# Last value rows over ACT in one transfer, the first value unit whole before the transposes, tiles copied by two engines

## The chip, the cores and the metric

One core of one Trainium2 chip. The metric is the device time of one execution in microseconds (us), as the median of several executions. The profile's own span is some 1.7 us shorter than that time (147.1 against 148.78 us for the profiled execution of the kernel before). I compare spans with spans and times with times.

Engines: PE is TensorE (PEld its weight loads), DVE is VectorE, ACT is ScalarE, POOL is GpSimd, SP is the engine that issues most transfers. PSUM is the memory that PE's results stand in until DVE or ACT copies them out.

## The reference

A token-wise gate mixes a linear attention branch and a feed-forward branch over 2048 tokens of width 448:

```python
g = sigmoid((x * gate_w).sum(-1, keepdims=True))
q, k, v = split_heads(x @ wqkv)                      # 16 heads of 28
phi_q = concat(softmax(q @ w_phi), softmax(-(q @ w_phi)))   # per head; phi_k from k in the same way
o = (phi_q @ (phi_k.T @ v)) / (phi_q @ phi_k.sum(tokens) + 1e-6)
a = o @ wo
b = gelu(x @ w1 + b1) @ w2 + b2
out = g * a + (1 - g) * b
# ... all inputs bfloat16; shapes: wqkv 448x1344, w_phi 16x28x28, w1 448x1792, w2 1792x448
```

## The kernel before

Only the first 14 us matter here. The value weights `WvG` (448 rows) are held as four chunks of 128 partitions; the last 64 rows are loaded twice, once into each half of chunk 3, because each half of the partitions serves one of two matmuls that run beside each other. The first 512 tokens of x are loaded as they are, in two blocks, and turned on PE (`turn`); everything else is turned by transposing transfers from SP. The key weights arrive transposed (`WkT`), are multiplied with a block matrix `bd` made of `w_phi` (`key_chunk`), and the result is the weight of the key units.

```python
nc.sync.dma_start(x0[:, 0:2, :], two[0])                       # first x block
nc.scalar.dma_start(WvG[:, 0:3, 0:D], ...)                     # value weights, 336 KB
nc.sync.dma_start(wphi[:, 0:3, :], ...)
nc.scalar.dma_start(wphi[0:HP, 3, :], wflat[384:448, :])       # HP = 64
nc.sync.dma_start(x0[:, 2:4, :], two[1])                       # second x block
# ...
for i in range(2):                                             # last value rows, into both halves
    nc.gpsimd.dma_start(WvG[i * HP:(i + 1) * HP, 3, 0:D], A_wqkv[384:448, 2 * D:3 * D])
# ...
load_wT(WkT, D, 0, 256)                                        # transposing transfers from SP
load_wT(WkT, D, 256, D)
load_x(512, 512)
load_wT(WqT, 0)
load_x(1024, 512)
# ...
turn(0, 1, nc.vector.tensor_copy, 0, 2)      # 4 PE transposes into PSUM, then one copy to xT
turn(0, 2, nc.scalar.copy, 2, 4)
turn(2, 0, nc.vector.tensor_copy)
idle(2, P)
v0a, v0b = V(0, 3), V(1, 0)                  # the first two value units: 6 full matmuls each
v0a.un.full(0, True, False)                  # 3 matmuls
v0a.un.full(1, True, False, cs=(0,))         # 1 matmul
turn(1, 1, nc.vector.tensor_copy)            # these two need the second x block
turn(3, 2, nc.scalar.copy)
for m in range(4):
    heads_map(m)                             # bd, on DVE
v0a.un.full(1, True, False, cs=(1, 2))       # the 2 matmuls left over
v0b.un.fulls(True, False)                    # needs tile 1, then tile 3
# ...
key_chunk(0, 1, nc.scalar.copy)              # needs WkT's first part and bd
key_chunk(1, 2, nc.scalar.copy)
v0a.un.rest(False, True)                     # needs the last value rows
v0b.un.rest(False, True)
key_chunk(2, 1, nc.vector.tensor_copy)       # needs WkT's second part
# ... the rest of the kernel
```

The softmax here doesn't subtract the row's maximum and nothing guards it: scores larger than these inputs give would overflow.

## Time and profile before

| | kernel before |
|---|---|
| time, median of 4 runs | 148.59 us (148.47 to 148.67) |
| span of the profiled execution | 147.1 us |
| PE busy | 97% |
| second x block: data moved / landed | 5.42 / 6.22 us |
| key weights' first / second part landed | 7.12 / 8.44 us |
| key weights' product starts on PE | 8.33 us |

"Landed" is the moment at which the last of the sixteen increments of a transfer's semaphore is recorded, one increment from each of the 16 DMA engines; that is what a waiting engine sees. The prediction shows the lines on which the argument rests. One view is added here: the busy times in stretches of 1 us. Its columns are the stretch, its length, the busy time of each engine, the granted clock, the mean busy share of the 16 DMA engines (packets that overlap are counted more than once, so it can exceed 1), and GB/s.

```profile
5.00:6.00 1.00, 0.82 (x4) 0.20 (x2) 0.09 (x1) 0.00 (x0) 1.00 (x1) 1.00 1.17 193
6.00:7.00 1.00, 0.73 (x10) 0.56 (x10) 0.30 (x1) 0.08 (x1) 1.00 (x3) 1.00 1.28 279
7.00:8.00 1.00, 1.00 (x7) 0.46 (x6) 0.95 (x5) 0.51 (x1) 1.00 (x2) 1.00 1.18 173
```

The DMA engines are busy all through these 3 us and move 173 to 279 GB/s.

### The profile page before, as it was taken

Reading aid. Unit: us, or ns where it says so; the run is one execution under the profiler, and the core shown is the slowest. Engines: PE = TensorE matmul, PEld = TensorE weight load, DVE = VectorE, ACT = ScalarE, POOL = GpSimd, SP = SyncE. Lnnn points to the kernel's source line nnn. Section 1 sums busy time; section 2 is a strip of 40 time slices with the busy share of each in tenths; the row PEclk is TensorE's granted clock in tenths of the full one; section 3 lists DMA queues with packets and bytes.
Section 4 is the critical chain, followed back from the end, with each engine's and each line's share of the span. In section 5 each row is a group of like instructions: output and inputs, shape, how many; then the busy total and the mean of one; then the engine's idle time right before and its main releaser. Section 6 shows DMA issues by size and latency. Waiting matters only on the chain.

```text
span 147.1 us, 3117 instructions
## 1 busy us (share of the span) xinstructions
PE 142.9 (97%) x1293; PEld 78.5 (53%) x1293; DVE 82.5 (56%) x140; ACT 64.8 (44%) x73; POOL 72.0 (49%) x59
## 2 busy tenths in 40 slices
PE   7899999999999999999999999999999999999992
PEld 4554645554566666964444445554555555545561
DVE  0342999997999992179993002721637747044112
ACT  4266987889999877326777762000000000000000
POOL 7932499898889999200699940000621110024000
PEclk9999999999999999999999999999999999999999
DMA  4999857449999999997159990340313623303111
GB/s 129 266 184 224 199 123 150 108 85 241 224 221 223 366 246 145 181 153 139 38 98 171 100 206 0 71 76 2 125 31 85 87 69 71 71 4 125 60 34 31
DMA packets 46190, 18.98 MB, mean 129 GB/s; under 512 B 36800, under 2 KB 46016, under 8 KB 46176
## 3 DMA queue, kind: packets, MB, share of 16 engines
q1 hardware_dynamic: 45392, 18.23, 61.8%
q10 hardware_dynamic: 624, 0.43, 0.9%
q8 instruction: 10, 0.16, 0.5%
q0 software_dynamic: 160, 0.12, 0.3%
q14 instruction: 4, 0.03, 0.1%
HBM read 6.34 MB, written 1.84 MB: 56 GB/s over the span
## 4 chain that ended last, share of the span: by engine, by line
PE 94%; DMA 3%; SPq 1%; DVE 0%; issue 0%
PE hp L478 29%; PE y L577 28%; PE q_ps L231 6%; PE y L194 6%; PE k_ps L231 4%; PE v_ps L194 3%; DMA gel<-in_A_x_dram 3%; PE v_ps L231 3%; PE kv L490 3%; PE nm L502 2%; PE k_ps L205 2%; PE k_ps L194 2%; PE w_ps L316 1%; PE y L211 1%; PE q_ps L194 1%; PE v_ps L211 1%
## 5 line engine op out<-in xcount | busy, mean ns | idle before, releaser
L577 PE MATMUL y<-w_sb,gel 128*128 128x448 bf16 (+1 forms) x224 | 43.8, 349 | 0.0
L478 PE MATMUL hp<-xT,w_sb 64*128 64x512 bf16 x224 | 42.7, 376 | 0.0
L478 PE MATMUL hp<-xS,w_sb 64*128 64x512 bf16 x168 | 40.1, 376 | 0.0
L482 ACT ACTIVATE gel<-hp,b1T 128x1024 bf16<-128x1024 f32 x28 | 30.8, 1115 | 13.6 <-PE hp L478 13.0
L478 PEld LDWEIGHTS <-w_sb 64*128 64x128 bf16 x392 | 22.9, 94 | 19.1
L577 PEld LDWEIGHTS <-gel 128*128 128x128 bf16 x238 | 22.3, 98 | 19.3 <-issue 0.4
L538 POOL TENSOR_SCALAR b2u<-b2b,ungate 128x448 f32<-128x448 bf16 x16 | 10.0, 642 | 40.2 <-DVE res L589 40.2
L259 POOL TENSOR_TENSOR gel<-gel,rec 128x1792 bf16<-128x1792 bf16 x8 | 25.6, 3214 | 2.2 <-DVE rec L258 2.2
L589 DVE SCALAR_TENSOR_TENSOR res<-y,ungate,b2u 128x448 bf16<-128x448 f32 (+1 forms) x16 | 10.3, 673 | 25.0 <-PE y L577 13.2
L259 POOL TENSOR_TENSOR phiq<-phiq,rec 128x1792 bf16<-128x1792 bf16 x4 | 12.7, 3211 | 11.0 <-DVE rec L258 11.0
L256 DVE TENSOR_REDUCE sums<-gel 128x64 f32<-128x1792 bf16 x8 | 16.0, 2002 | 0.0
L250 ACT ACTIVATE gel<-k_ps 128x896 bf16<-128x896 f32 x16 | 13.7, 922 | 3.5 <-PE k_ps L231 2.1
L509 DVE TENSOR_SCALAR den<-nm,enL 128x16 f32<-128x16 f32 x16 | 3.6, 228 | 17.0 <-PE nm L502 17.0
L231 PEld LDWEIGHTS <-xT 64*128 64x128 bf16 x112 | 9.2, 94 | 5.6 <-issue 0.4
L259 POOL TENSOR_TENSOR phqT<-phqT,rec 128x1792 bf16<-128x1792 bf16 x3 | 11.3, 3808 | 0.0
L515 DVE TENSOR_TENSOR o_all<-nm,den 128x448 bf16<-128x448 f32 (+2 forms) x24 | 11.0, 485 | 0.6
L231 PE MATMUL q_ps<-gel,xT 64*128 64x448 bf16 (+1 forms) x56 | 10.1, 349 | 0.0
L231 PEld LDWEIGHTS <-xS 64*128 64x128 bf16 x84 | 7.8, 94 | 3.8
L258 DVE RECIPROCAL rec<-sums 128x64 f32<-128x64 f32 x16 | 8.9, 553 | 1.1
L231 PE MATMUL q_ps<-phqT,xS 64*128 64x448 bf16 (+1 forms) x42 | 9.1, 349 | 0.0
L278 DVE CAST vaug<-v_ps 128x896 bf16<-128x896 f32 x7 | 7.5, 1070 | 2.7 <-PE v_ps L194 2.4
L194 PE MATMUL y<-wo_sb,phiq 128*128 128x448 bf16 (+1 forms) x36 | 8.2, 349 | 0.0
(96 smaller groups left out, 146.4 us busy)
## 6 DMA issues: line engine op xcount, KB each, us to landing
w_sb<-in_B_w_dram SPq DMA_DIRECT2D x4, 784.0 KB, 10.8
out_dram<-res SPq DMA_DIRECT2D x15, 112.0 KB, 1.7
w_sb<-in_B_w_dram SPq DMA_DIRECT2D x2, 560.0 KB, 13.6
xS<-xT SPq DMA_DIRECT2D x8, 96.0 KB, 2.3
phqT<-gel SPq DMA_DIRECT2D x4, 168.4 KB, 3.4
gel<-in_A_x_dram SPq DMA_DIRECT2D x2, 224.0 KB, 3.6
w_sb<-in_B_w_dram SPq DMA_DIRECT2D x1, 448.0 KB, 10.2
gel<-in_A_wqkv_dram ACTq DMA_DIRECT2D x1, 336.0 KB, 3.7
```

The lines of the kernel that those rows point to most:

```text
L194: nc.tensor.matmul(o, lhsT=self.L(i, slice(0, P), c), rhs=self.R(slice(0, P), c)[:, n0:n1], start=(first and c == 0), stop=(last and c == 2))
L231: nc.tensor.matmul(o, lhsT=tok, rhs=(W if direct else SWAPPED[name])[rows, c, 0:n], start=(k == 0), stop=own)
L250: nc.scalar.activation(out=o, in_=src, func=ACT.Exp, scale=(1.0, -1.0)[s])
L256: nc.vector.reduce_sum(out=sums[:], in_=ph, axis=AX.X)
L258: nc.vector.reciprocal(out=rec[:], in_=sums[:])
L259: eng.tensor_tensor(out=ph, in0=ph, in1=rec[:, :, :, None].to_broadcast([P, 32, 2, DH]), op=ALU.mult)
L478: nc.tensor.matmul(hp[:, i, :].rearrange("p (b t) -> p b t", b=2), lhsT=w1_sb[i * HP:(i + 1) * HP, k, j * P:(j + 1) * P], rhs=x_half(i, k, ...
L482: nc.scalar.activation(out=dst, in_=hp[:].rearrange("p i (b t) -> p i b t", b=2), func=ACT.Gelu_apprx_tanh, bias=b1T[:, j:j + 1])
L515: nc.vector.tensor_tensor(out=o_tok[:, col:col + (b - a) * DH].rearrange("p (q j d) -> p q j d", j=2, d=DH), in0=nm[:, a // 2:b // 2, 0:56 ...
L538: nc.gpsimd.tensor_scalar(out=b2u[t][:], in0=b2b[:], scalar1=ungate[:, place(t):place(t) + 1], scalar2=0.0, op0=ALU.mult, op1=ALU.add)
L577: nc.tensor.matmul(o, lhsT=gel[:, j, tok], rhs=w2_sb[:, j, n0:n1], start=(first and j == 0), stop=(last and j == NJ - 1))
L589: nc.vector.scalar_tensor_tensor(out=res[t][:, n0:n1], in0=o, scalar=ungate[:, e:e + 1], in1=b2u[t][:, n0:n1], op0=ALU.mult, op1=ALU.add)
```

## The change

The intent: take two transfers (1.3 us of issuing) off POOL by loading the last value rows twice in one transfer from ACT; fill the wait for the second x block with the two value matmuls that stood behind it; and have each of the two tiles that come with that block copied out of PSUM by DVE and ACT together, so that the second value unit can start sooner. Moved along with it: b1's small load and one SP issue less for `wo`.

```diff
@@ -119,6 +119,9 @@
     wflat = A_w_phi.rearrange("h a b -> (h a) b")
     nc.sync.dma_start(wphi[:, 0:3, :], wflat[0:384, :].rearrange("(c p) b -> p c b", p=P))
     nc.scalar.dma_start(wphi[0:HP, 3, :], wflat[384:448, :])
+    nc.scalar.dma_start(WvG[:, 3, 0:D],
+                        bass.AP(tensor=A_wqkv.tensor, offset=A_wqkv.offset + 384 * 3 * D + 2 * D,
+                                ap=[[0, 2], [3 * D, HP], [1, D]]))
     nc.sync.dma_start(x0[:, 2:4, :], two[1])
 
     def load_wT(W, base, r0=0, r1=D):
@@ -144,8 +147,6 @@
     nc.gpsimd.memset(ones[:], 1.0)
     nc.gpsimd.affine_select(out=ident[:], in_=ones[:], pattern=[[-1, P]],
                             compare_op=ALU.is_equal, fill=0.0, base=0, channel_multiplier=1)
-    for i in range(2):
-        nc.gpsimd.dma_start(WvG[i * HP:(i + 1) * HP, 3, 0:D], A_wqkv[384:448, 2 * D:3 * D])
     on4 = ones[:, 0:64].rearrange("p (c h) -> p c h", c=4)
     nc.gpsimd.affine_select(out=hm[:], in_=on4, pattern=[[P, 4], [-DH, 16]],
                             compare_op=ALU.is_ge, fill=0.0, base=0, channel_multiplier=1)
@@ -154,6 +155,7 @@
     nc.gpsimd.dma_start(gb[0:3, :], gate_w[0:384].rearrange("(c p) -> c p", p=P))
     nc.gpsimd.dma_start(gb[3:4, :].rearrange("o (i p) -> o i p", i=2),
                         gate_w[None, None, 384:448].to_broadcast([1, 2, HP]))
+    nc.gpsimd.dma_start(bb[0:NJ, :], B_b1.rearrange("(j p) -> j p", p=P))
     pk4 = phik.rearrange("p t (q m) -> p (t q) m", m=HP)
     nc.gpsimd.memset(pk4[:, :, 56:64], 0.0)
     nc.gpsimd.memset(vaug[:, :, :, 56:58], 1.0)
@@ -161,7 +163,6 @@
     nc.gpsimd.memset(pq4[:, :, 56:64], 0.0)
     pq4 = phiq[:].rearrange("p t (q m) -> p (t q) m", m=HP)
     nc.gpsimd.memset(pq4[:, :, 56:64], 0.0)
-    nc.gpsimd.dma_start(bb[0:NJ, :], B_b1.rearrange("(j p) -> j p", p=P))
 
     load_wT(WkT, D, 0, 256)
     load_wT(WkT, D, 256, D)
@@ -334,27 +335,28 @@
         for c in range(c0, c1):
             dlo = (0, 2, 1, 3)[j] * D + (c * P if c < 3 else (384 if j < 2 else 320))
             nc.tensor.transpose(tp[:, 0, c * P:(c + 1) * P], x0f[:, dlo:dlo + P], ident[:])
-        copy(out=xT[:, c0:c1, j * P:(j + 1) * P],
-             in_=tp[:, 0, c0 * P:c1 * P].rearrange("p (c t) -> p c t", t=P))
-
-    turn(0, 1, nc.vector.tensor_copy, 0, 2)
-    turn(0, 2, nc.scalar.copy, 2, 4)
-    turn(2, 0, nc.vector.tensor_copy)
+        for i, eng in enumerate(copy):
+            a, b = c0 + i * (c1 - c0) // len(copy), c0 + (i + 1) * (c1 - c0) // len(copy)
+            eng(out=xT[:, a:b, j * P:(j + 1) * P], in_=tp[:, 0, a * P:b * P].rearrange("p (c t) -> p c t", t=P))
+
+    both = (nc.vector.tensor_copy, nc.scalar.copy)
+    turn(0, 1, both[:1], 0, 2)
+    turn(0, 2, both[1:], 2, 4)
+    turn(2, 0, both[:1])
     idle(2, P)
     v0a, v0b = V(0, 3), V(1, 0)
-    v0a.un.full(0, True, False)
-    v0a.un.full(1, True, False, cs=(0,))
+    v0a.un.fulls(True, False)
+
     def heads_map(m):
         h0, h1 = HEADS[m]
         nc.vector.tensor_tensor(out=bd[:, m, 0:(h1 - h0) * DH].rearrange("p (h d) -> p h d", d=DH),
                                 in0=wphi[:, m, None, :].to_broadcast([P, h1 - h0, DH]),
                                 in1=hm[:, m, h0:h1, None].to_broadcast([P, h1 - h0, DH]), op=ALU.mult)
 
-    turn(1, 1, nc.vector.tensor_copy)
-    turn(3, 2, nc.scalar.copy)
+    turn(1, 1, both)
+    turn(3, 2, both)
     for m in range(4):
         heads_map(m)
-    v0a.un.full(1, True, False, cs=(1, 2))
     v0b.un.fulls(True, False)
     low_half(512, nc.gpsimd)
     twin(WqT, nc.gpsimd.tensor_copy)
@@ -422,8 +424,7 @@
         for i in range(2):
             f = slice(h * F // 2, (h + 1) * F // 2)
             nc.sync.dma_start(w1_sb[i * HP:(i + 1) * HP, :, f], B_w1[:, f].rearrange("(k p) f -> p k f", p=HP))
-    for c0, c1 in ((0, 1), (1, 3)):
-        nc.sync.dma_start(wo_sb[:, c0:c1, :], A_wo[c0 * P:c1 * P, :].rearrange("(c p) n -> p c n", p=P))
+    nc.sync.dma_start(wo_sb[:, 0:3, :], A_wo[0:384, :].rearrange("(c p) n -> p c n", p=P))
     for i in range(2):
         nc.sync.dma_start(wo_sb[i * HP:(i + 1) * HP, 3, :], A_wo[384:448, :])
     for j0, j1 in ((0, 5), (5, 10), (10, NJ)):
```

## The prediction

> **What bounds the kernel now.** I read the busy table first, then TensorE's (PE's) list of waits, then the chain that ended last, and only then the first 14 us of the timeline.
>
> ```profile
> PE 142.9 (97%) x1293; PEld 78.5 (53%) x1293; DVE 82.5 (56%) x140; ACT 64.8 (44%) x73; POOL 72.0 (49%) x59
> ...
> PE w_warm L322 <- PEq L640: 0.8, 1, 0.8
> PE tp L336 <- DMA gel<-in_A_x_dram: 0.4, 1, 0.4
> ```
>
> The first line is the busy table: PE is busy 97% of the span. The other two are all of PE's waits: the start, and 0.4 us for the second block of x before its transposes. Afterwards PE never waits for long enough to be listed, so a microsecond won or lost before about 14 us should reach the end of the kernel whole, unless a transfer further on takes it back. The chain says where such a microsecond can come from:
>
> ```profile
> 1.73 4.49 DMA gel<-in_A_x_dram
> 6.22 0.05 issue
> 6.27 0.62 PE tp L336 x8
> 6.88 1.61 PE v_ps L194 x8
> 8.49 0.46 PE w_ps L316 x8
> 8.95 0.48 PE v_ps L211 x4
> 9.44 0.34 PE w_ps L316 x4
> ```
>
> Columns are start, length, what. Until 6.22 us the chain is the second x transfer; from 6.27 it is PE alone: 8 transposes, 8 value matmuls (2 left of the first value unit, 6 of the second), the key weights' product for chunks 0 and 1 (w_ps), the last value rows (L211), then chunk 2. Details from the timeline:
>
> ```profile
> 4.89 0.93 PE L194 MATMUL v_ps<-gel,xT 128*128 128x448 bf16 x4
> 6.70 0.42 DVE L337 COPY xT<-tp 128x512 bf16<-128x512 bf16 x1 [1.61 <-PE tp L336]
> 6.92 0.59 ACT L337 COPY xT<-tp 128x512 bf16<-128x512 bf16 x1 [2.32 <-PE tp L336]
> 7.18 0.87 PEld L194 LDWEIGHTS <-xT 128*128 128x128 bf16 x6 [0.36 <-DVE xT L337]
> ```
>
> and from the list of transfers (size of one, us from issue to landing):
>
> ```profile
> gel<-in_A_wqkv_dram ACTq DMA_DIRECT2D x1, 336.0 KB, 3.7
> gel<-in_A_wqkv_dram POOLq DMA_DIRECT2D x2, 56.0 KB, 4.6
> gel<-in_A_wqkv_dram SPq DMA_TRANSPOSE x3, 4.9
> ```
>
> Value matmuls start about every 0.19 us (1.15 us for 6). Those of the first unit that stand before the transposes start at 4.89, 5.09, 5.28 and 5.47; a fifth could start at 5.66, but the transposes wait until 6.27. So the hole is 0.6 us of issue time, though the list shows 0.4, as it counts from the modelled end. The second unit starts at 7.18, when VectorE's (DVE's) whole-tile copy is done; the two left-over matmuls fill most of that wait. The last three lines are the bulk of the value weights over ACT, their last rows in two transfers over GpSimd (POOL), the transposed loads over SP. Of the latter the first two bring the key weights: issued at 2.25 and 3.7 they land at 7.1 and 8.4 (the landing events of the trace), for uses at 8.33 (chunk 0) and 9.37 (chunk 2). They have only 1.2 and 0.9 us to spare.
>
> **What the Trainium skill says.** (1) "DMA: Bandwidth & Descriptors", section "Issuing engines are not separate DMA queues": transfers from any issuer run on the same 16 DMA engines, so another issuer saves only the issuer's time. The trace agrees in that the 2 POOL transfers (1.34 us of POOL to issue) move their data in the midst of the second x block. (2) The same page, "Why a DMA increments its semaphore by 16 and not by 1": a transfer is spread over the largest k up to 16 that divides the slowest dimension (not of size 1) of both its access patterns, and one issued from SP or ACT takes the lowest-numbered k engines; "Rules for kernel authors" warns that a leading zero-stride broadcast of c copies confines a transfer to at most c engines. The new transfer is just that: its source as built is 2 copies (stride 0) of 64 rows, so k would be 2. No transfer from SP or ACT before has such a pattern, so this trace neither supports nor contradicts it. (3) "Queues, rings and completion order" there: an engine takes turns between the queues packet by packet. The trace records each 896-byte row as one packet (41 ns) and each transposed piece as a 256-byte packet (18 ns). (4) "TensorE: Matmul & The Clock Gate", Part 1: the clock drops only after an idle window of about 3.4 us. The granted clock is full here throughout, and the waits I expect are 1 us or less, so I count no clock loss.
>
> **The change part by part.**
> - *First value unit whole before the transposes.* Two matmuls (2 x 0.19 = 0.38 us) move into the 0.6 us hole. They issue until 6.04, so if x still lands at 6.22 the transposes still start at 6.27.
> - *Two engines per tile.* DVE's half tile is 256 columns: 0.29 us, as its copy of that size at 4.02 took, in place of 0.42. The copy of tile 1 starts 0.43 after the transposes' start T (6.27 to 6.70), so the second unit can start at T+0.43+0.29+about 0.07, i.e. T+0.79, against T+0.91. But the built program makes ACT's half wait for DVE's half of the same tile, not for PE. So the halves run one after the other: ACT's half (0.37 us, as at 4.23) ends at T+0.43+0.29+0.06+0.37, or T+1.15. The third matmul, which needs it, wants to go at T+0.79+0.38 = T+1.17: about 0.05 us late. Six matmuls end at about T+1.99; with T = 6.27 the key product could start at 8.26 in place of 8.33: **gain 0.07 us**. The head maps on DVE (0.91 us for 4) start at T+1.0, and the last one they delay is just in time.
> - *Last value rows from POOL to ACT.* This takes 112 KB out of the middle of the second x block. 112 KB at the 200 to 340 GB/s that the stretches from 3 to 6 us moved is 0.3 to 0.5 us, so x could land by 5.9 and T become 6.04: **another 0.23 us at most**. Together 0.1 to 0.3 us, if nothing else came of it.
> - *The other side of the same transfer.* With k = 2, two engines carry 64 rows each: 64 x 41 ns = 2.6 us, against 0.3 us (two POOL packets of 0.16) before. The SP transposes need all 16 engines, and the engines are nearly full from 5 us on. The first key transpose has 64 packets per engine; taking turns one for one with 64 rows costs it up to 2.6 us on these two engines, less the 0.3 saved and about 0.2 of idle time. It would land at about 7.1+2.1 = 9.2, the second at 8.4+2.1 = 10.5. The key product then starts at about 9.25, not 8.33: **+0.9 us**. Chunks 0 and 1 and the last rows take 1.04 us, so chunk 2 wants to start at 10.3 and waits to about 10.55: **+0.25 more**. Net of all, PE is 1.15 us later than before. Later transfers come about 2 us later on those engines too, but had more room: x's next block is first used at 13.0 after landing at 11.0, the query weights 2.3 us after 13.28, and both uses move by 1.15 as well.
> - *gate and b1 first, wo in one transfer.* POOL's head masks and small loads come 1.3 us sooner; gate's first use on PE is at 11.1, b1's at 17.7. wo is not used on PE before 99 us. One SP issue less of about 0.6 us. All hidden: 0.
>
> **The rivals.**
> - *A: the two-engine spread hits the key weights*, as summed: 148.55+1.15 = 149.7, say 149.3 to 150.2. For it: the pattern as built, the 0.9 and 1.2 us of spare time, the full engines. Against: nothing in this trace shows a spread of 2.
> - *B: the transfer is spread over 16 after all* (the pattern being turned round somewhere, or the destination's 128 rows deciding). Then only the gains remain: 148.55-0.07 to -0.3, i.e. 148.2 to 148.5. For it: the destination alone would give 16.
> - *C: spread over 2 but hidden*, the transposes going first and the rows creeping behind. Then the last value rows land late; they are wanted at 8.9, ahead of chunk 2, and would come at 8 to 10: 148.4 to 149.5. The PE wait then sits at L211's rows and not at w_ps.
> - *D: backlog*: the two loaded engines hold back later blocks (x at 13, the query weights at 15.5) more than the PE delay covers: 150.2 to 151.5.
>
> **How the range follows.** A 0.5, B 0.3, C 0.12, D 0.08. The middle of that mixture is about 149.5; from B's good half to A's bad end gives 148.2 to 150.3. None of these gets to 2% (below 145.6 or above 151.5), except a bad D. So within 2% has 0.95; faster 0.01, slower 0.04.
>
> **What the profile of the changed kernel would show.** A: PE's waits gain a wait of 0.7 to 1.2 us at w_ps for a DMA from wqkv, the key transposes' time to landing grows from 4.9 to about 7, and the new ACT transfer takes 6 us or more to land. B: that transfer lands within 5 us and the only PE wait left is 0.2 us or less at the transposes or the second value unit. In both: six value matmuls before the transposes, the transposes at 6.0 to 6.3, DVE's half copies at 0.29 us, and ACT's halves starting only after DVE's. From 23 us on every stretch should be as long as before, merely shifted; a difference there would make the working wrong even if the total were right. A landing of x much later than 6.3 would mean that the rows collide with x rather than with the transposes.

## The result, and the profile after

The changed kernel takes **150.43 us** (median of 4 runs, 150.12 to 150.80) against 148.59 us before: it is slower by 1.25% (ratio 1.0125, 95% interval 1.0101 to 1.0150). The prediction said 149.5 with a range up to 150.3, so the time fell just outside. "Within 2%" held.

The busy table of the kernel after, and then PE's waits (who waited for what: us in total, times, longest):

```profile
PE 143.6 (97%) x1293; PEld 74.6 (50%) x1293; DVE 85.3 (57%) x141; ACT 64.8 (44%) x74; POOL 70.5 (47%) x57
```

```profile
PE tp L337 <- DMA gel<-in_A_x_dram: 1.2, 1, 1.2
PE w_warm L323 <- PEq L641: 0.8, 1, 0.8
PE v_ps L195 <- DVE xT L340: 0.2, 1, 0.2
```

The busy table alone says nothing: PE is at 97% as before. The list of waits tells where to look: the wait for the second x block grew from 0.4 to 1.2 us, and a small wait for DVE's copy appeared. There is no wait for the key weights, which the prediction had named as the place: they landed at 9.51 us, 0.4 us before PE came to them (9.90). The chain that ended last, after:

```profile
1.73 6.17 DMA gel<-in_A_x_dram
7.91 0.05 issue
7.95 0.41 PE tp L337 x4
8.36 0.02 issue
8.39 0.30 DVE xT L340
8.69 0.05 issue
8.73 1.33 PE v_ps L195 x6
10.07 0.46 PE w_ps L317 x8
```

The x transfer, issued at the same 1.73, lands at 7.91 instead of 6.22. From there to the key product (10.07 against 8.49 in the chain's reckoning) the chain is 0.1 us shorter than before. The product is 1.58 us late, and the span 1.5 us longer (148.6 against 147.1). Later stages add nothing: from the first hidden-layer matmul to PE's last it is 103.4 us before (40.91 to 144.29) and 103.3 us after (42.49 to 145.82).

The stretches that answer to those of before:

```profile
5.00:6.00 1.00, 1.00 (x4) 0.33 (x4) 0.09 (x1) 0.00 (x0) 1.00 (x3) 1.00 3.34 83
6.00:7.00 1.00, 0.78 (x4) 0.21 (x2) 0.00 (x0) 0.00 (x0) 1.00 (x2) 1.00 0.14 47
7.00:8.00 1.00, 0.05 (x1) 0.05 (x2) 0.00 (x0) 0.00 (x0) 0.56 (x1) 1.00 1.13 98
```

Here is the loss. Between 6 and 7 us the DMA engines are busy to 0.14 of 16, which is about 2 engines, and move 47 GB/s where they moved 279 before. The 3.34 in the stretch before is no high load: it counts packets in full where they start, and 24 packets of the key weights' transposed load, which start between 5.06 and 5.61 us, take 1.6 to 2.2 us each (the trace's packet records; they end between 7.17 and 7.31, and 18 ns is usual). The packet records do not name the engine, but 0.14 of 16 engines and the late increments below fit one reading: fourteen engines stand still with a transposed packet in hand, and two work.

The list of transfers, after (size, us to landing):

```profile
gel<-in_A_wqkv_dram ACTq DMA_DIRECT2D x1, 336.0 KB, 3.7
gel<-in_A_wqkv_dram ACTq DMA_DIRECT2D x1, 112.0 KB
gel<-in_A_wqkv_dram SPq DMA_TRANSPOSE x3, 6.2
```

The new 112 KB transfer has no time to landing, because its semaphore does not count in sixteen single steps. The trace has three updates for it: one at 3.28 us, before any of its rows had moved, and one each at 8.39 and 8.70. Two engines did the work, as the prediction had expected from the pattern. Its 128 rows, one packet each, moved between 4.71 and 8.05 us.

And the x block: its last data packet ended at 5.14 us, even sooner than before (5.42). Its sixteen increments came at 5.15 and 5.25 us from two engines, and between 7.60 and 7.91 from the other fourteen. **The bytes had been there for 2.8 us before PE was told so.** The trace also has sixteen packets of 4 bytes on SP's queue between 4.57 and 5.14 us, as many as there are increments. If these are the writes of the increments, as their number and place suggest, even they had been started by then.

From the timeline, after, the parts that went as planned (start, length, engine, line, operation; in brackets the idle time before and what ended it):

```profile
4.89 1.88 PE L195 MATMUL v_ps<-gel,xT 128*128 128x448 bf16 x6
8.39 0.51 DVE L340 COPY xT<-tp 128x256 bf16<-128x256 bf16 x2 [3.30 <-PE tp L337]
8.71 0.65 ACT L340 COPY xT<-tp 128x256 bf16<-128x256 bf16 x2 [4.10 <-DVE xT L340]
```

Six value matmuls stand before the transposes. The copies are halves, and ACT's start only when DVE's first half is done. (That six matmuls took 1.88 us and not 1.3 is told in the next section but one.)

### The profile page after: what moved, and what is told of

It is laid out like the page before. It is cut to its first block, busy times and chain, and to the rows that moved or that the text cites. A ratio compares the mean times of both kernels' runs of the same rounds, so it can differ in the third digit from the quotient of the medians.

```text
span 148.6 us, 3116 instructions
## 1 busy us (share of the span) xinstructions
PE 143.6 (97%) x1293; PEld 74.6 (50%) x1293; DVE 85.3 (57%) x141; ACT 64.8 (44%) x74; POOL 70.5 (47%) x57
## 3 DMA queue, kind: packets, MB, share of 16 engines
HBM read 6.34 MB, written 1.84 MB: 55 GB/s over the span
## 4 chain that ended last, share of the span: by engine, by line
PE 93%; DMA 4%; SPq 1%; DVE 0%; issue 0%
PE hp L479 29%; PE y L578 28%; PE q_ps L232 6%; PE y L195 6%; DMA gel<-in_A_x_dram 4%; PE k_ps L232 4%; PE v_ps L195 3%; PE v_ps L232 3%; PE kv L491 2%; PE nm L503 2%; PE k_ps L206 2%; PE k_ps L195 2%; PE w_ps L317 1%; PE y L212 1%; PE q_ps L195 1%; PE v_ps L212 1%
## 5 line engine op out<-in xcount | busy, mean ns | idle before, releaser
L479 PE MATMUL hp<-xS,w_sb 64*128 64x512 bf16 x168 | 40.7, 376 | 0.0
L479 PEld LDWEIGHTS <-w_sb 64*128 64x128 bf16 x392 | 18.8, 94 | 23.2
L260 POOL TENSOR_TENSOR phqT<-phqT,rec 128x1792 bf16<-128x1792 bf16 x3 | 9.6, 3210 | 0.0
(95 smaller groups left out, 150.3 us busy)
```

Of the source, the lines that this page charges most:

```text
L260: eng.tensor_tensor(out=ph, in0=ph, in1=rec[:, :, :, None].to_broadcast([P, 32, 2, DH]), op=ALU.mult)
L479: nc.tensor.matmul(hp[:, i, :].rearrange("p (b t) -> p b t", b=2), lhsT=w1_sb[i * HP:(i + 1) * HP, k, j * P:(j + 1) * P], rhs=x_half(i, k, ...
```

## The experiments

**Theories.** S (spread): the last value rows sit on two DMA engines, and that alone costs the time. Q (queue): a third transfer on ACT's queue delays x, however it is spread. P (order): PE's new order and the shared copies cost. Within S there is a second question, why x was late at all: X says that x's completion is held on the fourteen other engines by transposed packets that cannot proceed; R says that the rows, or any transfer next in the queue, hold it.

### Sixteen engines, and by accident four times: e1_k16, e1_k8, e1_k4, e1_k2

The changed kernel with the rows still over ACT, but as two transfers of 64 rows. The small tail of `w_phi` goes to POOL, so that ACT has no fourth transfer. The other three were to have 8, 4 and 2 engines.

```diff
-    nc.scalar.dma_start(WvG[:, 3, 0:D], bass.AP(..., ap=[[0, 2], [3 * D, HP], [1, D]]))
+    for i in range(2):
+        nc.scalar.dma_start(WvG[i * HP:(i + 1) * HP, 3, 0:D], A_wqkv[384:448, 2 * D:3 * D])
     # e1_k8, e1_k4, e1_k2 (k = 8, 4, 2): the source as ap=[[64 // k * 3 * D, k], [3 * D, 64 // k], [1, D]]
```

> The changed kernel with its last value rows still over ACT, but as two transfers of 64 rows each (built as 64 rows on both sides, so a spread over 16 DMA engines, 8 rows each); the small tail of w_phi goes to GpSimd, so that ACT has no fourth transfer. Theory S (the spread over 2 engines is the cause): the second x block lands at 5.6 to 6.0 us instead of 7.9, the transposes start at 6.0 to 6.1, the key product at about 8.0, and the time is 148.1 to 148.5 us, 0.1 to 0.4 below before. Rival Q (a third transfer on ACT's queue is what holds x, however it is spread): x lands after 7 us and the time stays at 150 to 150.5. Rival P (the new order on TensorE and the shared copies cost): x lands early but the time stays above 149.5.

> As the 16-engine run, but each 64-row transfer written as 8 blocks of 8 rows, so that it should use 8 engines with 16 rows each. Theory S, with about 55 ns for a row on a loaded engine from about 4.6 us on (as in the changed kernel's trace: 64 rows per engine end at 8.05): rows end at about 5.5, x lands at 5.6 to 6.1, time 148.1 to 148.6. Rival Q: 150 to 150.5 as for any spread.

> As the 16-engine run, but each transfer written as 4 blocks of 16 rows: 4 engines, 32 rows each. Theory S: rows end at about 6.4, x lands at 6.1 to 6.6, the key transposes about 0.8 us later than in the 16-engine run; time 148.4 to 148.9. Rival Q: 150 to 150.5.

> As the 16-engine run, but each transfer written as 2 blocks of 32 rows: 2 engines, 64 rows each, without any zero stride in the pattern. Theory S: as the changed kernel, x lands at 7.5 to 8.2 and the time is 150.0 to 150.7. If it is the zero stride or the single transfer that costs and not the number of engines, x lands by 6.2 and the time is below 148.8.

Blocks of rows that lie one after another are merged into 64 rows when the kernel is built. So these are four runs of one program with 16 engines, and my expectations for e1_k8, e1_k4 and e1_k2 say nothing. They serve as a measure of noise instead: 148.65, 148.76, 148.80 and 148.58 us (medians; single runs 148.33 to 149.34) against 148.57 before; ratios 1.0009, 1.0001, 1.0010 and 1.0002. In the four profiled executions x landed at 5.90, 6.21, 6.30 and 5.99 us and the key product started, in the chain, at 8.07, 8.37, 8.47 and 8.16.

From e1_k16's list of transfers, and then from its stretches:

```profile
gel<-in_A_wqkv_dram ACTq DMA_DIRECT2D x2, 56.0 KB, 4.1
```

```profile
6.00:7.00 1.00, 0.84 (x11) 0.51 (x10) 0.62 (x3) 0.29 (x2) 1.00 (x3) 1.00 1.28 280
```

The rows land within 4.1 us, and the stretch from 6 to 7 us moves 280 GB/s again. Both transfers have their sixteen increments in all four traces, so the spread is 16. With everything else of the change in place the loss is gone: that speaks against Q and P. But the expected gain of 0.1 to 0.4 us is not there either. The first of the four looked good in its profile (146.6 us span), the others less so; x's landing alone varies by 0.4 us between executions of one program, and a gain of 0.1 us cannot be seen under that.

### A real spread of 2 and of 4: p2_rows, p4_rows

To keep the builder from merging, the source takes the rows in a permuted order, so **the results are wrong** (relative errors 0.45 and 0.47). The amount of work is the same, and the tail of `w_phi` is on POOL as in e1_k16.

```diff
+    for i in range(2):
+        nc.scalar.dma_start(WvG[i * HP:(i + 1) * HP, 3, 0:D],
+                            bass.AP(..., ap=[[3 * D, k], [k * 3 * D, 64 // k], [1, D]]))     # k = 2, 4
```

> The first four runs turned out to be one program (blocks of rows that lie one after another are merged into 64 rows when the kernel is built), so their spread was 16 in all. Here the source takes the rows in a permuted order, 2 rows outermost, which is not merged: two transfers of 64 rows on ACT, each on 2 engines, 64 rows for each engine in all. The value rows come in a wrong order, so the result is wrong on purpose. Theory S (number of engines): as the changed kernel, x lands at 7.5 to 8.2 us, the time is 150.0 to 150.8. If the zero stride or the one transfer of 128 rows is what costs, x lands by 6.4 and the time is 148.4 to 149.0.

> As the last, with 4 rows outermost: 4 engines, 32 rows for each (wrong result on purpose). Theory S, with about 55 ns for a row on a loaded engine from about 4.6 us on: the rows end at about 6.4, x lands at 6.2 to 6.7 and the time is 148.6 to 149.2, between 16 engines (148.58 to 148.80 in four runs of one program) and 2 engines (150.4). A threshold at any spread under 16 would give 150 or more.

Two engines: 150.15 us (149.97 to 150.53; ratio 1.0094, 1.0077 to 1.0111). The data of x ended later here (6.19 us), it landed at 7.57 instead of 7.91 (fourteen of the sixteen increments had come by 7.05), the key weights at 9.99, and 23 transposed packets took over 1 us. That two engines did the work shows in the semaphores again: one early update and two late ones for each of the two transfers (four late ones for each in p4_rows). So it is neither the zero stride nor the single transfer: two engines are enough. But PE waited twice here:

```profile
PE tp L338 <- DMA gel<-in_A_x_dram: 0.7, 1, 0.7
PE w_ps L318 <- DMA gel<-in_A_wqkv_dram: 0.3, 1, 0.3
```

The wait that ended last is the one for the key weights, the place that the prediction had named: they landed at 9.99, and the key product started at 10.03. Four engines: 149.11 us (148.89 to 149.23; ratio 1.0026, 1.0011 to 1.0041). The longest transposed packet up to 15 us took 0.77 us and x landed at 6.03, both as with sixteen engines (0.70 to 0.98 and 5.90 to 6.30 in the four runs above); the key weights landed at 8.08, later than there (7.27 to 7.43). The time lies between, as S says for a smaller dose. But p4's profiled run does not show x as the wait: there the six value matmuls took 2.05 us instead of 1.3 (a late clock, below). How much of its 0.3% is the spread stays open.

### The one part alone: e2_k2_only

The kernel before, with only the rows' transfer changed.

```diff
-    for i in range(2):
-        nc.gpsimd.dma_start(WvG[i * HP:(i + 1) * HP, 3, 0:D], A_wqkv[384:448, 2 * D:3 * D])
+    nc.scalar.dma_start(WvG[:, 3, 0:D], bass.AP(..., ap=[[0, 2], [3 * D, HP], [1, D]]))     # ahead of the second x block
```

> The kernel before with one edit: the last value rows over ACT in the one transfer on 2 engines instead of over GpSimd; TensorE's order and the copies are as before. Theory S: x lands at 7.6 to 8.2 and the time is 150.3 to 150.9, as slow as the whole change or 0.1 slower. Rival P (TensorE's new order and the shared copies carry a part of the loss): below 150.0.

150.47 us (150.21 to 151.70; ratio 1.0136, 1.0092 to 1.0179). The slowest of the four had a granted clock of 0.989; the other three lie between 150.21 and 150.62. This one edit is the whole loss, within the noise. In its profile x landed at 7.42, a little sooner than I had expected.

### All but that part: e3_rows_pool

The changed kernel with the rows back on POOL in two transfers.

```diff
-    nc.scalar.dma_start(WvG[:, 3, 0:D], bass.AP(..., ap=[[0, 2], [3 * D, HP], [1, D]]))
+    for i in range(2):                                                   # on POOL, ahead of the head masks, as before
+        nc.gpsimd.dma_start(WvG[i * HP:(i + 1) * HP, 3, 0:D], A_wqkv[384:448, 2 * D:3 * D])
```

> The changed kernel with its last value rows back on GpSimd in two transfers, as before: the new order on TensorE, the shared copies, gate and b1 first and wo in one transfer stay. Theory S (nothing but the spread of the rows cost time; the rest gains 0.07 us by the sum of the prediction): x lands at 6.0 to 6.4, the key product starts at 8.2 to 8.4, time 148.3 to 148.8. Rival P (the rest costs): over 149.2.

148.84 us (148.54 to 149.00; ratio 1.0004, 0.9985 to 1.0023). The rest of the change neither costs nor gains anything that can be measured. That rules out P.

### The issuer: e11_k2_pool

The kernel before with the zero-stride transfer, but issued by POOL.

```diff
-    for i in range(2):
-        nc.gpsimd.dma_start(WvG[i * HP:(i + 1) * HP, 3, 0:D], A_wqkv[384:448, 2 * D:3 * D])
+    nc.gpsimd.dma_start(WvG[:, 3, 0:D], bass.AP(..., ap=[[0, 2], [3 * D, HP], [1, D]]))
```

> The kernel before with its last value rows in one transfer with the zero stride, but still issued by GpSimd. If the pattern decides the spread for GpSimd as well (2 engines, 64 rows each), the other engines' transposed packets stall and x lands after 7: 150 to 151. If GpSimd spreads the 128 rows over 16 engines all the same, x lands by 6.4 and the time is 148.4 to 148.8.

149.95 us (149.79 to 150.31; ratio 1.0088, 1.0070 to 1.0106). x landed at 7.80. PE's wait in its list:

```profile
PE tp L337 <- DMA gel<-in_A_x_dram: 2.1, 1, 2.1
```

The 128 rows went in 26 packets of four or five rows, about two at a time, between 5.04 and 7.71. Here ten of x's sixteen increments had come by 5.74, and only six were late (6.83 to 7.80); 19 transposed packets took over 1 us. The pattern does it with either issuer, and with two transfers on ACT as before, so Q is not needed.

### What holds x: e6_plain_behind

The changed kernel, with a plain 784 KB transfer (a block of the first-layer weights, issued later in the kernel otherwise) between the second x block and the key weights' transposed loads on SP's queue.

```diff
+    nc.sync.dma_start(w1_sb[0:HP, :, 0:F // 2], B_w1[:, 0:F // 2].rearrange("(k p) f -> p k f", p=HP))
     load_wT(WkT, D, 0, 256)
```

> The changed kernel, with a plain transfer of a first-layer weight block (784 KB) put on SP's queue between the second x block and the key weights' transposed loads, instead of later. Theory X (x's bytes have long arrived, but its completion is held on the other 14 engines by transposed packets that stall behind the 2 loaded engines): with plain packets next in the queue, x lands by 6.4, although the rows still run until about 8; the key weights land 2 to 4 us later than in the changed kernel, and the time is 151 to 154. Rival R (the rows themselves hold x, or any transfer behind x is held the same way): x still lands after 7.4.

One look, 154.67 us. The state of a single run is unknown, and the time lies just past what I had expected. What was asked is in its PE waits and then in its stretches:

```profile
PE w_ps L318 <- DMA gel<-in_A_wqkv_dram: 4.0, 1, 4.0
```

```profile
8.00:9.00 1.00, 0.78 (x4) 0.20 (x2) 0.43 (x3) 0.07 (x1) 0.00 (x0) 1.00 1.90 185
9.00:10.00 1.00, 0.00 (x0) 0.00 (x0) 0.00 (x0) 0.00 (x0) 0.00 (x0) 1.00 1.96 75
10.00:11.00 1.00, 0.00 (x0) 0.00 (x0) 0.00 (x0) 0.00 (x0) 0.00 (x0) 1.00 0.16 44
```

PE's wait for x is gone from the list: x landed at 6.16 us, although the two engines worked on the rows until 11.62 (later than the 8 us I had put down, since the plain transfer shares these engines). Fifteen of its increments had come by 5.52. So neither the rows nor just any transfer next in the queue holds x, and R is ruled out, as far as one execution can do it. Then, with the transposed loads next, the same picture as in the changed kernel appears some 3.7 us later: 0.16 busy, 44 GB/s, 21 transposed packets that start from 8.79 on and end at about 11.0. The stall goes with the transposed packets, and x's completion is late only where those come right behind it: X. After the 4 us without work PE's clock was down as well: the clock records show half speed from 13.05 to 16.47 us, and the mean granted clock of this run is 0.989, where the other profiled runs have 0.999 or 1. So part of its time is not the transfers'.

### A better order: e10_x_first and e9_best

If x's landing sets the start, x should be issued sooner. e10 is the kernel before with two lines exchanged; e9 adds rows on 16 engines over ACT and the shared copies. (e9 was made from the changed kernel, so b1's earlier load and the single transfer of `wo` are in it as well, and the tail of `w_phi` is on POOL.)

```diff
     nc.sync.dma_start(x0[:, 0:2, :], two[0])
     # ...
+    nc.sync.dma_start(x0[:, 2:4, :], two[1])
     nc.sync.dma_start(wphi[:, 0:3, :], ...)
-    nc.sync.dma_start(x0[:, 2:4, :], two[1])
     # e9: and e1_k16's rows, `turn(1, 1, both)` and `turn(3, 2, both)`, and v0a's matmuls 4 before and 2 after
```

> The kernel before with one edit: the second x block is issued ahead of w_phi on SP's queue, 0.46 us sooner. If x's landing is what the start waits for, x lands at 5.6 to 5.9, the transposes start up to 0.5 us sooner (not before 5.66, when the four value matmuls ahead of them are issued), time 148.0 to 148.4. If the engines are full anyway and x lands at 6.1 or later all the same: 148.5 to 148.7.

> Put together: rows over ACT in two 64-row transfers (16 engines), second x block ahead of w_phi, four value matmuls before the transposes and two after (as before), both engines copying each tile (as in the change). By the sums: transposes at 5.7 to 5.9, second value unit at 6.5 to 6.8 instead of 7.18, key product at 7.65 to 7.95 instead of 8.33; time 147.9 to 148.3, below both kernels. If the key weights' transposed loads (7.0 to 7.3) or the clock's late rise take it back: 148.4 to 148.8.

e10: **148.34 us** (148.25 to 148.42; ratio 0.9976, 0.9961 to 0.9991), below both kernels. x landed at 5.46 instead of 6.22, and PE no longer waits for it: its only wait is the one at the start. From its chain:

```profile
4.96 1.15 PE v_ps L194 x4
6.11 0.45 PE tp L336 x8
6.56 1.60 PE v_ps L194 x8
8.16 0.46 PE w_ps L316 x8
```

The four matmuls took until about 6, not 5.7 (a late clock again, by their spacing), so 0.3 of the 0.8 us that x gained arrives.

e9: 149.09 us (148.97 to 149.31; ratio 1.0028, 1.0013 to 1.0043), a miss. Its PE waits:

```profile
PE w_ps L316 <- DMA gel<-in_A_wqkv_dram: 0.4, 1, 0.4
```

The last of the key weights' first part landed at 8.42, after 7.12 before, so the second of the two outcomes I had written down came, and stronger. That transfer became the bound. Neither part alone shows this in its profiles: with x ahead (e10) the key weights landed at 7.07, with the rows on ACT (the four runs of one program) at 7.27 to 7.43. That x and the rows together pushed them back is a guess; which of e9's parts did it was not tried.

## Why the prediction was wrong, point by point

**The bound: right.** A delay before 14 us does go through whole: 1.58 us at the key product, 1.5 us at the end.

**The spread over two engines: right**, though nothing in the trace before could show it. It came from the Trainium skill, page "DMA: Bandwidth & Descriptors", section "Why a DMA increments its semaphore by 16 and not by 1". The semaphore with one early update and two late ones agrees (3.28, 8.39, 8.70 us), and p2_rows and e11_k2_pool show that the pattern decides, not the zero stride or the issuer.

**PE's side: right.** The second unit was to start at T+0.79 and end at T+1.99, with T the start of the transposes; with T = 7.95 it started at T+0.78, and the key product followed at T+1.95 (9.90). ACT's halves did wait for DVE's. That this part gains only 0.07 us fits the chain, which is 0.1 us shorter from x to the product; e3_rows_pool shows that the time can neither confirm nor refute so small a gain.

**Gate, b1 and wo: right**, hidden (e3_rows_pool holds them as well).

**The delay of the key weights: nearly right in size, not in how it came.** Their first part was to land at 9.2 us and did so at 9.51; the second was to land at 10.5 and came sooner, at 9.90. The new transfer landed at 8.70, 6.7 us after its issue, as rival A had it (6 us or more). But the sum let rows and transposed packets take turns one for one, and only on the two loaded engines. In the trace 65 rows start between 5.75 and 7.0 us and only 5 transposed packets on all engines together. That two engines with 64 rows each set the delay either way made the sum come out; that much is luck.

**The step that failed** is in the third part of the prediction, "Last value rows from POOL to ACT": "x could land by 5.9 and T become 6.04". I took a transfer to have landed when its data has moved, and counted only the other work on each DMA engine, as if the fourteen engines without rows would go on. The data did move by 5.14 us, as the step said. But fourteen of the sixteen increments came at 7.60 or later, because the transposed packets right behind x stood still on those engines. So the first wait was not at the key product (9.25 in the sum) but at the transposes (7.95). From there PE still had 1.95 us of work up to the product. Hence 9.90 in place of 9.25.

How much of the loss is x's late landing, and how much the path that the prediction had named? The key weights' first part landed at 9.51, so with x on time the product could have started at about 9.55 (an estimate: p2_rows has 0.04 us between that landing and the product). Of the 1.57 us by which the product moved, some 1.2 would have come through the key weights alone, and x's hold put 0.35 on top. Without it the time would be about 150.1 (the measured 150.43 less 0.35), close to rival A's 149.7. The other terms between 149.7 and the 150.43 measured are smaller: the key weights landed 0.3 us later than summed, and the quarter of a microsecond that A adds for their second part did not come, since its use was at 10.95. The last 0.3 us is not traced to a stage: the medians differ by 1.84 us, the two profiled executions by 1.62.

The prediction did name a sign for this case, "a landing of x much later than 6.3 would mean that the rows collide with x rather than with the transposes", and even that reading was half wrong. e6_plain_behind shows that the rows alone leave x in peace; it takes the transposed packets behind it. And the transposes were hit as well. None of the four rivals had x's completion as the wait, so the range ended at 150.3.

**The clock** is a smaller omission, and "the granted clock is full here throughout" was a misreading. I counted 0.19 us for each of the six first matmuls. After the change they took 1.88 us instead of 1.3, since in that execution they still ran at about 0.37 us each up to some 6 us; it was hidden by the wait for x. In e1_k16 the same six took 1.30 us. The Trainium skill's page "TensorE: Matmul & The Clock Gate" (Part 1) says that the moment at which the clock rises varies from run to run. The trace's clock records agree: full speed from 4.96 us before, 6.12 us after, 3.65 to 4.55 us in the four runs of one program. The stretches' clock column shows 1.00 for this time all the same; one sees it only by the spacing of PE's instructions (before: transposes 0.11 us apart at 3.6 to 4.2 us, 0.06 us from 6.27 on).

**What stays open.** Why transposed packets stand still on all engines when two are behind was not tried. That they need all engines in step is a guess. Five profiles show the stall at the start with two loaded engines (the changed kernel, p2_rows, e2_k2_only, e6_plain_behind and e11_k2_pool); with the rows on sixteen, no transposed packet up to 15 us takes longer than 0.98 us. But two loaded engines are not the only occasion. In the kernel before, later transposing transfers stall six times in the same way (at 53, 57, 64, 70, 83 and 117 us; packets of 0.9 to 1.5 us that end together), and five of the six begin while a single 16 KB packet of the kind "instruction" (one packet, so one engine) is under way (0.92 to 1.32 us). That fits the guess and does not prove it. How far p4_rows' 0.3% is the spread is open as well.

## What to carry to other kernels

Before giving a transfer a repeated source in its outermost dimension, look at how many DMA engines it will use: a small transfer on two engines took 1.8 us from a kernel in which its own data was never waited for. Take a transfer's end from its semaphore's increments and not from its bytes, and ask what comes right behind it in the queue. And look at the built pattern of an experiment before the run, or four experiments may turn out to be one.

## What the Trainium skill lacked or had wrong

- "DMA: Bandwidth & Descriptors", section "Rules for kernel authors": of a transpose next to ordinary transfers it says that it "needs nothing", which is about correctness; that it can cost time is missing. Here, beside an ordinary transfer on two engines, transposed packets stood still: 24 of them took 1.6 to 2.2 us instead of 18 ns, and the engines moved 47 GB/s instead of 279.
- The same page, "Queues, rings and completion order": it explains that a completion waits for earlier writes. It does not say that a completion can wait while packets from behind it in the queue stall: x's data had moved by 5.14 us and x landed at 7.91, but at 6.16 when plain packets came next (one execution).
- The same page, "Rules for kernel authors": one row advises one 128-partition transfer in place of two to the halves, another warns of a leading zero stride. Where the halves get the same rows, the two rows pull apart. Here two transfers took 148.58 to 148.80 us and the one took 150.43.
- No page has it: blocks of rows that adjoin are merged when a kernel is built, so a pattern written with 2, 4 or 8 blocks of rows outermost ran as 64 rows (sixteen increments in each trace; 148.58 to 148.80 us).
